# A Fourier mixing and squared-ReLU FFN kernel: self-mirrored frequencies as single tokens, and the odd DFT sums in a PSUM bank of their own

## The chip, the cores and the metric

The kernel runs on one core of a Trainium2 chip. The time is the device time of one execution in microseconds (us); what is compared is the median of several executions. A profile of one execution stands beside it: its span runs from the first to the last instruction and is a little shorter than the device time.

The core has five engines that take their instructions in program order and wait for one another by semaphores. TensorE (PE) does the matmuls and writes into the accumulator memory, PSUM, which this kernel uses as eight banks of 512 float32 columns on 128 partitions. ScalarE (ACT) and VectorE (DVE) read PSUM, do the elementwise work and write to the on-chip memory, SBUF. GpSimd (POOL) does some elementwise work from SBUF to SBUF. SyncE (SP) issues most of the transfers.

## The reference

```python
x: [8, 3008, 256]; w_in: [256, 2048]; w_out: [2048, 256]      # float32
X = np.fft.fft(np.fft.fft(x, axis=1), axis=2).real            # mix over sequence and features
t = X.reshape(8 * 3008, 256)                                  # 24064 tokens
h = np.maximum(t @ w_in, 0.0)
out = (h * h) @ w_out
```

The input is real, so the output rows of the frequencies k and 3008 - k of a batch come from the same two sums, one cosine sum P and one sine sum Q over the sequence: one row is P + Q after the feature transform, the other is P - Q. The kernel works on such a pair as a "plus" token and a "minus" token. The frequencies 0 and 1504 are mirrored to themselves.

## The kernel before

The sizes: M = 1504 is half the sequence, QN = 752, NE = 753 even and NO = 752 odd frequencies from 0 to 1504, so NK = 1505 pairs for each of 8 batches.

**First stage.** The input is folded on DVE, and then a DFT of length 752 is done as matmuls with cosine and sine tables, in two blocks (even and odd frequencies), for each of P (`pt`) and Q (`qt`). A block is a sum over six slices: slices 0, 2, 4 give a sum A, slices 1, 3, 5 a sum B. The lower half of a block's frequencies is A + B; the upper half is B - A (or A - B), read backwards.

```python
def dft_ops(blk, mms, m, fin, run=3):
    ...
        def f():
            ms = mms(par)                                  # par 0: slices 0, 2, 4; par 1: slices 1, 3, 5
            if lo == 0 and par == 0:
                st[0] = psx.tile([P, 512], F32, name="pf", tag="x")[:, 0:n]      # one PSUM bank
            for i in range(lo, hi):
                rows, wt, q, tab = ms[i]
                mm(st[0][0:rows, :], wt(q), tab[k, q, c0 : c0 + n], par == 0 and i == 0, i == len(ms) - 1)
            if hi < len(ms):
                return
            if par == 0:
                st["a"] = asp.tile([P, HE], F32, name="as", tag="as")[:, 0:n]
                act(st["a"][0:m, :], st[0][0:m, :], AF.Copy, bias=0.0,
                    scale=2.0 if fin[0] is None else fin[0])                     # 2A to SBUF
            else:
                fin[1](st["a"][0:m, :], st[0][0:m, :])                           # bank now holds A + B
...
            def f(a2, lo):                                 # fin of stage1_ops
                act(lo_, lo, AF.Copy, bias=0.0, scale=1.0)                       # lower half: ACT copies A + B
                ...
                    vt(hi_, a2, lo, op=ALU.subtract)                             # upper half: DVE
```

The matmuls of the odd slices add onto the even ones' sum in the same bank, and so they come after ACT's copy of 2A. The first block of batch 0 (`stage1_first`) already has its sums in two banks.

**Second stage.** The pairs of all batches are cut into 25 chunks (two of 256 pairs, 22 of 512, and the last of 264), and each chunk into steps over the 2048 hidden features. A step makes a PSUM tile `xb` of pre-activations; ACT applies ReLU for the plus tokens; the minus tokens are made in one of five ways, which a table of letters (KINDS) picks for each step. The kinds "r" and "v" add a third pass over the columns on PE (with the matrix G3) and finish on ACT (r) or DVE (v). The kinds "d", "q" and "p" do without it and build a correction tile T instead: d on DVE; q with a copy on ACT and an add on POOL; p with the edge term X on POOL; all three finish with one custom DVE instruction. The squaring of `h` goes to DVE, or to ACT where a second table (SQA) says so.

```python
def x_take(c, u):                                          # first half of d, q, p
    ...
    if KINDS[c][u] == "q":
        act(T, xb, AF.Copy, bias=0.0, scale=-2.0)
        for i in range(0, n, CH // 2):
            w = slice(i, i + CH // 2)
            nc.gpsimd.tensor_tensor(T[:, w], T[:, w], X[:, w], op=ALU.add)
    else:
        stt(out=T, in0=xb, scalar=-2.0, in1=X, op0=ALU.mult, op1=ALU.add)
...
def x_back(cur):                                           # second half: r and v
    for j in range(nf):
        for (b, i, o, l) in segs:
            mm(xb[:, j, o : o + l], G3[:, fs], PQ[b][1][:, i : i + l], False, True)
```

**Output.** For each tile of 128 tokens 16 matmuls (128 x 128 by 128 x 256) sum over the hidden features into `po`; ACT evicts it to `os`; SP stores the rows. A chunk's output matmuls are spread among the steps of the following chunks. The last chunk has 264 pairs: two tiles of plus tokens, two of minus tokens, and one tile that holds the 8 remaining pairs of both sides.

```python
def mm2_ops(c):
    full = n // P * P
    tiles = [(s, t0, P) for s in range(2) for t0 in range(0, full, P)]
    groups = [tiles[i : i + 2] for i in range(0, len(tiles), 2)]
    if n > full:
        groups.insert(0, [(2, full, n - full)])            # the tile of both sides
    ...
        w = MW if s == 2 else m                            # MW = 65 columns
        mm(st["o"][0:w, j, :], h2v(c, fc // nf)[:, fc % (2 * nf), o : o + w], wout16[:, fc, :],
           fc == 0 and j == 0, fc == NFC - 1)
```

In `rows_out` the minus rows of the frequencies 0 and 1504 are computed and left unstored.

PSUM is shared out as six banks for `xb`, `pf` and the weight products (`psx`) and two for `po` (`pso`).

Of the kernel before, what the change touches and what calls it, by code (L numbers as in the profile page):

```python
# [18 lines left out]
HS = 32.0  # L19
# [5 lines left out]
def kernel(  # L25
# [19 lines left out]
    NK = NE + NO  # L45
    HE = QN // 2 + 1
# [135 lines left out]
    sgn2 = vec("sgn2")  # L182
# [13 lines left out]
    def sgn_vecs():  # L196
        nc.gpsimd.tensor_scalar(out=sgn, in0=pidx, scalar1=P - 1.5, scalar2=None, op0=ALU.is_lt)
        nc.gpsimd.tensor_scalar(out=s3, in0=sgn, scalar1=-2.0, scalar2=None, op0=ALU.mult)
        nc.gpsimd.tensor_scalar(out=sgn, in0=sgn, scalar1=2.0, scalar2=-1.0, op0=ALU.mult, op1=ALU.add)
        nc.gpsimd.tensor_scalar(out=nsgn, in0=sgn, scalar1=-1.0, scalar2=None, op0=ALU.mult)  # L200
        nc.gpsimd.tensor_scalar(out=sgn2, in0=sgn, scalar1=2.0, scalar2=None, op0=ALU.mult)
# [192 lines left out]
    def alloc_pq(b):  # L394
        PQ[b] = tuple(pp.tile([P, NK], F16, name=n, tag=n) for n in ("pt", "qt"))

    def halves(blk, d):
        if blk == 0:
            return d[:, 0:HE], d[:, NE - 1 : HE - 2 : -1]
        return d[:, NE : NE + HO], d[:, NK - 1 : NE + HO - 1 : -1]  # L400

    def dft_ops(blk, mms, m, fin, run=3):
# [4 lines left out]
        def some(par, lo, hi):  # L407
            def f():
                ms = mms(par)
                if lo == 0 and par == 0:  # L410
                    st[0] = psx.tile([P, 512], F32, name="pf", tag="x")[:, 0:n]
                for i in range(lo, hi):
                    rows, wt, q, tab = ms[i]
                    mm(st[0][0:rows, :], wt(q), tab[k, q, c0 : c0 + n], par == 0 and i == 0,
                       i == len(ms) - 1)
                if hi < len(ms):
                    return
                if par == 0:
                    st["a"] = asp.tile([P, HE], F32, name="as", tag="as")[:, 0:n]
                    act(st["a"][0:m, :], st[0][0:m, :], AF.Copy, bias=0.0,  # L420
                        scale=2.0 if fin[0] is None else fin[0])
                else:
                    fin[1](st["a"][0:m, :], st[0][0:m, :])
# [7 lines left out]
    def stage1_ops(b, blk, inline_e=False, run=3):  # L431
# [12 lines left out]
        def fin(sn):  # L444
            def f(a2, lo):
                hi = P - 1 if sn and not inline_e else P
                lo_, hi_ = halves(blk, PQ[b][sn][0:hi])
                act(lo_, lo, AF.Copy, bias=0.0, scale=1.0)
                if sn and inline_e:
                    stt(out=hi_, in0=lo, scalar=nsgn[:, 0:1], in1=a2, op0=ALU.mult, op1=ALU.add)  # L450
                elif sn:
                    vt(hi_, a2, lo, op=ALU.subtract)
                else:
                    vt(hi_, lo, a2, op=ALU.subtract)
            return f

        ops = []
        for sn in range(2):
            ops.append(dft_ops(blk, lists(sn), P - 1 if sn and not inline_e else P,
                               (sgn2[:, 0:1] if sn and inline_e else None, fin(sn)), run))  # L460
        h = [len(o) // 2 for o in ops]
        return ops[0] + ops[1]
# [36 lines left out]
    def e_ops(bs):  # L499
# [7 lines left out]
        def fin(blk):  # L507
            def f(a2, lo):
                lo_, hi_ = halves(blk, est[bs[0]][0][0:nb])
                act(lo_, lo, AF.Copy, bias=0.0, scale=1.0)  # L510
                vt(hi_, lo, a2, op=ALU.subtract)
            return f

        ops = []
        for blk in range(2):
            ops.append(dft_ops(blk, lambda par, blk=blk: [
                (MW, lambda q: ewide((blk * NQ + q) * B + bs[0]), q, cosT)
                for q in range(par, NQ, 2)], nb, (None, fin(blk))))
        return [start] + [o[i] for i in range(2) for o in ops]

    def e_row(b):
        t, i = est[b]
        nc.sync.dma_start(out=PQ[b][1][P - 1 : P, :], in_=t[i : i + 1, :])

    NPAIR = B * NK
# [3 lines left out]
    assert all(n <= CH // 2 or n == CH or n % P < P // 4 for n in sizes)  # L529
    chunks = []  # L530
    g = 0
    for n in sizes:
        segs = []
        o = 0
        while o < n:
            b, i = divmod(g + o, NK)
            l = min(n - o, NK - i)
            segs.append((b, i, o, l))
# [3 lines left out]


    KINDS = ["vrvrrrvrrrrrrrrr"] + ["rvvrvrvrrrrrrrrr"] + ["rvrrvvrrvvvrrrrr"] + ["rrrrrrrrdqqdrrrr"] + ["rdrqdrqdrrrvdrrd"] + ["rrrrdqrrqrqdrqqd"] + ["rrrrrrqqqddrdrqd"] + ["rrdrqpdrpdqrrrqr"] + ["drpddrqrpdqrdrdr"] + ["qdqrqrdrvrddqdrr"] + ["ddrqddprrrddrqdr"] + ["qrqddrqdrrddqprr"] + ["drrdrddrrdpqdrdr"] + ["rqqdrdrqrqqrqddq"] + ["qrdddrqrqdpqqqdq"] + ["rrrrrrqqqddqrdrq"] + ["ddddqrqpqdpqdqrr"] + ["ppdrqdrqrdqdvqqr"] + ["qdqqdqrqrqdqdqvq"] + ["drqddqrddrdqrqpq"] + ["dpdqddqqrrdrqddr"] + ["qdqqdqrdqrqdrdqr"] + ["qdqddqrrdrqdrdqr"] + ["qdqqdqvrqrqdqrdp"] + ["rrppddpddddrppdp"]
    SQA = [(2,)] * 2 + [(1, 6)] + [(1, 4)] + [(0, 2, 3, 5)] + [(0, 6)] + [(1, 3, 7)] + [(2, 6)] + [(0, 2, 5, 7)] + [(0, 2, 4, 7)] + [(3, 7)] + [(0, 2, 4, 6)] + [(0, 2, 5)] + [(2, 4, 6)] + [(1,)] + [(1, 4, 6, 7)] + [(1, 2, 6)] + [(1, 4, 6)] * 2 + [(0, 5, 6, 7)] + [(1, 4, 6)] * 3 + [(1, 4, 6, 7)] + [(0, 1, 2, 6)]

    LEAD = ["2222222222222222"] * 3 + ["2222222246222222"] + ["2325322822222228"] + ["2222462222242224"] + ["2222222262122228"] + ["2252248522227232"] + ["5262823222223242"] + ["2622222222258222"] + ["2272622222222262"] + ["4223722222225622"] + ["2227223222628222"] + ["2226222221228242"] + ["6224422722233722"] + ["2222222282272322"] + ["4222222526636622"] + ["2225222212222242"] + ["8223822222422222"] + ["2242642242482252"] + ["2224282822222222"] + ["2822222222282222"] + ["2222222222222222"] + ["2282222222222222"] + ["2262232122422275"]
    DEFER = ["1111111111111111"] * 3 + ["1111111311131111"] + ["1101011111112111"] + ["1111221111111111"] + ["1111111111111111"] + ["1121113111111111"] + ["1112111111131111"] + ["1111211111121211"] + ["1121111111111121"] + ["1111211311111111"] + ["1111111111111111"] + ["1122101111111211"] + ["1111011111111131"] + ["1111111110111111"] + ["1111111011111111"] + ["1111101211111111"] + ["1111111111211111"] + ["1211101111111010"] + ["1111111111111111"] + ["1111211121131111"] + ["1111311211111111"] + ["1111111111111111"] + ["1101111101113111"]
    SQLAG = ["1111"] + ["3103"] + ["31123133"] + ["33343343"] + ["33332333"] + ["42331333"] + ["33331433"] + ["33333323"] + ["33344033"] + ["33323223"] + ["33333333"] + ["33333233"] * 2 + ["13333022"] + ["33333314"] + ["33333312"] + ["34333333"] + ["32333333"] + ["33232313"] + ["33133133"] + ["33333333"] + ["33233333"] + ["33333333"] + ["33323333"] + ["33334332"]
# [20 lines left out]
    def mm2_ops(c):  # L570
        g0, n, nf, segs = chunks[c]
        full = n // P * P
        tiles = [(s, t0, P) for s in range(2) for t0 in range(0, full, P)]
        groups = [tiles[i : i + 2] for i in range(0, len(tiles), 2)]
        if n > full:
            groups.insert(0, [(2, full, n - full)])
# [3 lines left out]
        def rows_out(s, t0, m, src):  # L580
            base = g0 + n - t0 - m if s else g0 + t0
            o = 0
            while o < m:
                b, i = divmod(base + o, NK)
                if i < NE:
                    l = min(m - o, NE - i)
                    kk = 2 * i
                else:
                    l = min(m - o, NK - i)
                    kk = 2 * (i - NE) + 1  # L590
                lo, hi = 0, l
                if s and kk == 0:
                    lo = 1
                if s and kk + 2 * (l - 1) == M:
                    hi = l - 1
                if hi > lo:
                    if s:
                        r0 = b * S + S - (kk + 2 * (hi - 1))
                        p0 = m - (o + hi)
                    else:  # L600
                        r0 = b * S + kk + 2 * lo
                        p0 = o + lo
                    nl = hi - lo
                    nc.sync.dma_start(out=out[r0 : r0 + 2 * nl - 1 : 2, :], in_=src(p0, nl))
                o += l

        def store(grp, po, js=None):
            os_ = osp.tile([P, 2, D], F32, name="os", tag="os")
            if grp[0][0] == 2:
                _, t0, m = grp[0]  # L610
                act(os_[0 : 2 * m, 0], po[0 : 2 * m, 0], AF.Copy, bias=0.0, scale=HS * HS)
                rows_out(0, t0, m, lambda p0, nl: os_[p0 : p0 + nl, 0, :])
                rows_out(1, t0, m, lambda p0, nl: os_[m + p0 : m + p0 + nl, 0, :])
                return
            js = js or slice(0, len(grp))
            act(os_[:, js], po[:, js], AF.Copy, bias=0.0, scale=HS * HS)  # L616
            for j, (s, t0, m) in list(enumerate(grp))[js]:
                rows_out(s, t0, m, lambda p0, nl, j=j: os_[p0 : p0 + nl, j, :])

        def one(grp, j, fc):  # L620
            s, t0, m = grp[j]

            def f():
                if j == 0 and fc == 0:
                    st["o"] = pso.tile([P, 2, D], F32, name="po", tag="po")
                o = n + n % P + t0 if s == 1 else t0
                w = MW if s == 2 else m
                mm(st["o"][0:w, j, :], h2v(c, fc // nf)[:, fc % (2 * nf), o : o + w], wout16[:, fc, :],
# [14 lines left out]
    def relu_d(c, u, put):  # L643
        n, nf = chunks[c][1:3]
        o = u % 2 * nf
        d = h2v(c, u)[:, o : o + nf, n : 2 * n]
        k = n % P
        if k:
            put(d[:, :, 0:k][:, :, ::-1], slice(0, k))
            put(d[:, :, k:n][:, :, ::-1], slice(k, n))  # L650
# [315 lines left out]
```

## Time and profile before

| what | value |
|---|---|
| time, median of 3 (lowest to highest) | 605.47 us (605.43 to 607.0) |
| span of the profiled execution | 603.7 us |
| mean granted PE clock | 0.994 of full speed |
| output matmuls (`po`, 256 columns) | 3024, 450.4 us busy |
| DFT matmuls (`pf`) in all | 240 |
| ACT copies of even sums (`as`, line 420) | 34, 0.46 to 0.63 us each |
| ACT copies of lower halves (`pt`, `qt`, `es`, lines 448 and 510) | 34, about 0.5 us each |
| DVE subtractions for upper halves (lines 450, 452, 454, 511) | 34, about 0.55 us each |
| squarings of 128 x 2048: DVE / ACT (two halves) | 116 at 1.23 us / 68 at 1.10 + 1.08 us |

Busy time is the sum of an engine's instruction durations. PE's matmuls overlap one another by their run-out, so PE's pace is read from the distance between starts and not from the mean duration of a matmul. "Idle before" is the time an engine stood still just ahead of an instruction, and the releaser is the instruction whose semaphore ended it. PE loads the weights of the next matmul beside the running one; those loads are listed as PEld.

### The profile page before, as it was taken

The page shows a single profiled execution, that of the slowest core. Times are in us where ns is not written, and L with a number is a line of the kernel's source. Part 1 is how long each engine was busy: PE and PEld are TensorE (multiplying, and loading weights), DVE is VectorE, ACT ScalarE, POOL GpSimd, SP SyncE. Part 2 cuts the span into 40 slices and gives each one's busy share as a digit, 9 for nine tenths or more (in the row PEclk, how much of TensorE's full clock was granted, in tenths as well). Part 3 has the DMA queues.
Part 4 walks back from the last instruction along what each step waited for, and adds up shares of the span by engine and source line. Part 5 has one row for each costly group of instructions (what it writes and reads, how often), then busy time and mean ns, then how long its engine had stood idle before and what let it go on. Part 6 is the DMA issues. An engine that isn't in the chain of part 4 may idle for free.

```text
span 603.7 us, 12339 instructions
## 1 busy us (share of the span) xinstructions
PE 579.6 (96%) x4539; PEld 436.3 (72%) x4539; DVE 523.4 (87%) x950; ACT 544.8 (90%) x976; POOL 188.3 (31%) x256
## 2 busy tenths in 40 slices
PE   3869899999999999999999999999999999999997
PEld 1546577777777777777787778777787778877786
DVE  7969698998799899988998988988989889899880
ACT  7868799999989899989999989998999899999981
POOL 6301022223231232323104354153453434324400
PEclk9979999999999999999999999999999999999999
DMA  8974755673584313913133115123242231332112
GB/s 251 298 75 111 157 156 180 210 188 102 56 226 88 44 55 54 256 44 57 46 54 62 35 55 53 54 44 58 58 55 48 42 61 54 44 62 56 55 54 71
DMA packets 41954, 56.25 MB, mean 93 GB/s; under 512 B 7746, under 2 KB 36726, under 8 KB 41894
## 3 DMA queue, kind: packets, MB, share of 16 engines
q1 hardware_dynamic: 37030, 42.04, 32.1%
q0 software_dynamic: 4864, 13.44, 9.0%
q8 instruction: 35, 0.57, 0.4%
q14 instruction: 25, 0.20, 0.1%
HBM read 29.02 MB, written 24.64 MB: 89 GB/s over the span
## 4 chain that ended last, share of the span: by engine, by line
PE 92%; DMA 4%; ACT 1%; POOL 1%; issue 1%; DVE 1%; POOLq 0%; ACTq 0%; DVEq 0%
PE po L74 54%; PE xb L74 31%; PE pf L74 6%; DMA wout<-in_moe_w_out_dram 3%; DMA x<-in_x_dram,idx 1%; POOL x L99 0%; POOL x L112 0%; ACT as L420 0%; ACT os L616 0%; ACT h L726 0%; DVE w L375 0%; DVE v L371 0%; ACT h L747 0%; DVE sinT L304 0%; DVE cosT L304 0%
## 5 line engine op out<-in xcount | busy, mean ns | idle before, releaser
L74 PE MATMUL po<-wout,h 128*128 128x256 f16 x3024 | 450.4, 273 | 4.8 <-DMA wout<-in_moe_w_out_dram 4.3
L74 PEld LDWEIGHTS <-h 128*128 128x128 f16 x3024 | 286.8, 98 | 113.5 <-issue 5.6
L714 POOL TENSOR_TENSOR bs<-bs,h 128x256 f32<-128x256 f32 x190 | 141.0, 764 | 289.3 <-ACT bs L711 225.4
L74 PE MATMUL xb<-qt,G 128*128 128x512 f16 (+10 forms) x737 | 205.2, 322 | 0.4 <-DVE qt L487 0.3
L727 DVE CUSTOM_DVE_ANT_0 h<-xb,bs 128x512 f16<-128x512 f32 (+1 forms) x237 | 147.9, 638 | 19.6 <-ACT h L726 14.9
L726 ACT ACTIVATE h<-xb 128x512 f16<-128x512 f32 (+1 forms) x224 | 139.4, 625 | 11.6 <-PE xb L74 9.9
L74 PE MATMUL xb<-pt,G 128*128 128x512 f16 (+16 forms) x512 | 146.7, 324 | 0.6 <-ACT h L738 0.3
L750 DVE TENSOR_TENSOR h<-h 128x2048 f16<-128x2048 f16 (+1 forms) x120 | 144.6, 1209 | 0.2
L74 PEld LDWEIGHTS <-G 128*128 128x128 f16 x1249 | 119.9, 98 | 23.8 <-issue 1.7
L669 ACT ACTIVATE h<-xb 128x512 f16<-128x512 f32 (+1 forms) x160 | 100.2, 630 | 8.9 <-PE xb L74 8.5
L716 DVE SCALAR_TENSOR_TENSOR bs<-xb,h 128x512 f32<-128x512 f32 (+1 forms) x129 | 84.9, 659 | 17.6 <-PE xb L74 13.9
L738 ACT ACTIVATE h<-xb 128x512 f16<-128x512 f32 (+2 forms) x145 | 89.7, 621 | 6.7 <-PE xb L74 5.2
L748 ACT ACTIVATE h<-h 128x1024 f16<-128x1024 f16 (+1 forms) x72 | 77.4, 1076 | 0.0
L747 ACT ACTIVATE h<-h 128x1024 f16<-128x1024 f16 (+1 forms) x72 | 76.3, 1059 | 0.1
L695 DVE TENSOR_SCALAR h<-eb,gE 128x512 f16<-128x512 f16 (+1 forms) x203 | 69.5, 360 | 0.3 <-DMA eb<-qt 0.2
L616 ACT ACTIVATE os<-po 128x512 f32<-128x512 f32 (+1 forms) x95 | 59.6, 627 | 8.9 <-PE po L74 8.9
L711 ACT ACTIVATE bs<-xb 128x512 f32<-128x512 f32 x95 | 59.6, 627 | 2.0 <-DVE h L727 1.0
L112 POOL DMA_INDIRECT x<-in_x_dram,idx x16 | 18.2, 1138 | 80.4 <-DVE u L366 63.3
L362 DVE TENSOR_TENSOR u<-x 127x765 f16<-127x765 f32 x32 | 29.7, 948 | 1.2 <-DMA x<-in_x_dram,idx 1.2
L74 PEld LDWEIGHTS <-w 127*128 127x128 f16 (+1 forms) x192 | 21.7, 117 | 8.4 <-issue 2.5
L375 DVE TENSOR_TENSOR w<-v 127x384 f16<-127x384 f16 x64 | 23.0, 383 | 0.0
L74 PE MATMUL pf<-cosT,w 127*128 127x377 f16 (+1 forms) x96 | 20.6, 323 | 2.2 <-ACT as L420 1.1
(111 smaller groups left out, 216.9 us busy)
## 6 DMA issues: line engine op xcount, KB each, us to landing
out_dram<-os SPq DMA_DIRECT2D x157, 128.0 KB
x<-in_x_dram SPq DMA_DIRECT2D x16, 756.0 KB
wst<-in_moe_w_in_dram SPq DMA_DIRECT2D x4, 512.0 KB
eb<-qt SPq DMA_DIRECT2D x14, 128.0 KB
wout<-in_moe_w_out_dram POOLq DMA_DIRECT2D x4, 256.0 KB, 17.3
x<-in_x_dram,idx POOLq DMA_INDIRECT x20, 10.5
gE<-G SPq DMA_DIRECT2D x16, 0.2 KB
x<-in_x_dram SPq DMA_DIRECT2D x14, 2.0 KB
```

What stands on the lines that cost most here:

```text
L74: nc.tensor.matmul(o, l, r, start=start, stop=stop, skip_group_check=True)
L616: act(os_[:, js], po[:, js], AF.Copy, bias=0.0, scale=HS * HS)
L669: act(r_s(c, u), xb, AF.Relu, scale=-1.0)
L695: ts(out=X, in0=ebc[c][:, 0:n], scalar1=gE2[:, u : u + 1], scalar2=None, op0=ALU.mult)
L714: nc.gpsimd.tensor_tensor(T[:, w], T[:, w], X[:, w], op=ALU.add)
L716: stt(out=T, in0=xb, scalar=-2.0, in1=X, op0=ALU.mult, op1=ALU.add)
L726: act(r_s(c, u), xb, AF.Relu, scale=-1.0)
L727: mirrors.append((int(DEFER[c][u]), lambda: relu_d(c, u, lambda o, i: nc.vector._custom_dve(TENSOR_ADD_SAT, out=o[:, 0, :], in0=xb[:, 0, i ...
L738: relu_d(c, u, lambda o, i: act(o, xb[:, :, i], AF.Relu, scale=-1.0))
L747: act(h2[:, 0:nf], h2[:, 0:nf], AF.Square)
L748: rest.append(lambda: act(h2[:, nf:], h2[:, nf:], AF.Square))
L750: vt(h2, h2, h2, op=ALU.mult)
```

## The change

Two things are changed, and the tables that place the work are set anew.

First, the frequencies 0 and 1504 of every batch are taken out of the pairs. Their columns of P and Q are copied aside by POOL (`self_copy`), and the 16 columns of the 8 batches are put behind the pairs of the last batch (`self_append`), as plus tokens without a minus token. The pairs are now 1503 for each batch; the last chunk has 248 pairs and 16 single tokens, 512 tokens in all. The odd tile of both sides and its handling go.

Second, the odd sums of a DFT get a bank of their own. ACT still copies A (now with scale 1, or with a sign) to SBUF; DVE makes both halves, A + B and B - A, and ACT's copy of the lower half goes.

Beside these, POOL's add of a "q" step is one instruction over 512 columns in place of two, and KINDS, SQA, three tables of delays and the places of the folds and DFTs among the steps are changed.

```diff
-    def halves(blk, d):
+    selfs = [const.tile([P, NS], F16, name=n) for n in ("ptS", "qtS")]        # NS = 16
+    def self_copy(b):
+        for sn in range(2):
+            hi = P - 1 if sn and b not in INL else P
+            nc.gpsimd.tensor_copy(selfs[sn][0:hi, 2 * b : 2 * b + 2], PQ[b][sn][0:hi, 0 : NE : NE - 1])
+    def self_append():
+        for sn in range(2):
+            nc.gpsimd.tensor_copy(PQ[B - 1][sn][:, NT : NT + NS], selfs[sn])
+    def halves(blk, d, o=None):                 # the odd block now begins at column NE - 1
 ...
     def dft_ops(blk, mms, m, fin, run=3):
-                if lo == 0 and par == 0:
-                    st[0] = psx.tile([P, 512], F32, name="pf", tag="x")[:, 0:n]
+                if lo == 0:
+                    st[par] = psx.tile([P, 512], F32, name="pf", tag="x")[:, 0:n]
-                    mm(st[0][0:rows, :], wt(q), tab[k, q, c0 : c0 + n], par == 0 and i == 0,
+                    mm(st[par][0:rows, :], wt(q), tab[k, q, c0 : c0 + n], i == 0,
                        i == len(ms) - 1)
-                        scale=2.0 if fin[0] is None else fin[0])
+                        scale=1.0 if fin[0] is None else fin[0])
-                    fin[1](st["a"][0:m, :], st[0][0:m, :])
+                    fin[1](st["a"][0:m, :], st[1][0:m, :])
 ...
-            def f(a2, lo):
+            def f(a, bp):
-                act(lo_, lo, AF.Copy, bias=0.0, scale=1.0)
                 if sn and inline_e:
-                    stt(out=hi_, in0=lo, scalar=nsgn[:, 0:1], in1=a2, op0=ALU.mult, op1=ALU.add)
-                elif sn:
-                    vt(hi_, a2, lo, op=ALU.subtract)
+                    stt(out=lo_, in0=a, scalar=sgn[:, 0:1], in1=bp, op0=ALU.mult, op1=ALU.add)
+                    later(lambda: stt(out=hi_, in0=bp, scalar=nsgn[:, 0:1], in1=a, op0=ALU.mult,
+                                      op1=ALU.add))
                 else:
-                    vt(hi_, lo, a2, op=ALU.subtract)
+                    vt(lo_, a, bp, op=ALU.add)
+                    if sn:
+                        vt(hi_, a, bp, op=ALU.subtract)
+                    else:
+                        later(lambda: vt(hi_, bp, a, op=ALU.subtract))
 ...
     def e_row(b):
-        nc.sync.dma_start(out=PQ[b][1][P - 1 : P, :], in_=t[i : i + 1, :])
+        nc.sync.dma_start(out=PQ[b][1][P - 1 : P, 0 : NE - 1], in_=t[i : i + 1, 0 : NE - 1])
+        nc.sync.dma_start(out=PQ[b][1][P - 1 : P, NE - 1 : NT], in_=t[i : i + 1, NE:NK])
+        nc.sync.dma_start(out=selfs[1][P - 1 : P, 2 * b : 2 * b + 2], in_=t[i : i + 1, 0 : NE : NE - 1])
-    NPAIR = B * NK
+    NPB = NT - 1                                # 1503
+    NPAIR = B * NPB + NS
 ...
     def mm2_ops(c):
-        full = n // P * P
-        tiles = [(s, t0, P) for s in range(2) for t0 in range(0, full, P)]
+        n1 = mirrored(c)                        # n, less 16 in the last chunk
+        tiles = list(range(0, n + n1, P))
-        if n > full:
-            groups.insert(0, [(2, full, n - full)])
 ...
-            for i in range(0, n, CH // 2):
-                w = slice(i, i + CH // 2)
-                nc.gpsimd.tensor_tensor(T[:, w], T[:, w], X[:, w], op=ALU.add)
+            nc.gpsimd.tensor_tensor(T, T, X, op=ALU.add)
 ...
     warm_up(10)
+    gcast(0, nc.scalar.copy)
     hi_ops = []
     s1 = stage1_first(hi_ops)
     s1[0]()
     warm_up(0)
-    gcast(0, nc.scalar.copy)
 ...
-    spread(fo, 12, 13)
+    spread(fo, 9, 10)
     spread(tr1[0:5], 12, 13)
-    spread(tr1[5:], 12, 13)
+    spread(tr1[5:], 11, 12)
-    FOLD = {0: [(1, 0.511, 0.793)], ...
+    FOLD = {0: [(1, 0.475, 0.842)], ...         # the fold of batch 1, as shares of batch 0's steps
-    ST1 = {0: (0.9, 0.99)}
+    ST1 = {0: (0.843, 0.905)}                   # the DFT of batch 1
+    side.setdefault(first_step[B - 1] + 5, []).append(self_append)
```

The tables, summed over all 400 steps (and, for SQA, over all pairs of steps):

| | r | v | d | q | p | squarings on ACT |
|---|---|---|---|---|---|---|
| before | 158 | 18 | 108 | 95 | 21 | 72 |
| after | 168 | 14 | 106 | 92 | 20 | 79 |

## The prediction

> **What bounds the kernel now.** I read the page first, for the share of each engine and the slices; then the busy time by stretch, to see where TensorE (PE) is not full; then PE's waits, which name what it stood for; then PE's timeline of two places, the end of the start-up and the tail.
>
> From the page (busy time and share of the span; then the same in 40 slices, in tenths):
> ```profile
> PE 579.6 (96%) x4539; PEld 436.3 (72%) x4539; DVE 523.4 (87%) x950; ACT 544.8 (90%) x976; POOL 188.3 (31%) x256
> ...
> PE   3869899999999999999999999999999999999997
> ```
> The stretches (length, then busy time and number of instructions of PE, PEld, DVE, ACT, POOL):
> ```profile
> 36.00:75.00 39.00, 35.79 (x235) 24.26 (x234) 29.00 (x58) 29.13 (x56) 2.23 (x2) 0.95 0.51 108
> 75.00:150.00 75.00, 75.00 (x587) 54.17 (x585) 70.55 (x128) 71.39 (x128) 21.50 (x24) 1.00 0.57 168
> 150.00:300.00 150.00, 150.00 (x1200) 112.21 (x1198) 134.02 (x230) 140.15 (x245) 40.53 (x51) 1.00 0.44 92
> 300.00:450.00 150.00, 150.00 (x1206) 115.69 (x1204) 134.32 (x235) 140.60 (x251) 57.32 (x78) 1.00 0.30 53
> ```
> From 75 us to 580 us PE has no gap: that part lasts as long as its matmuls, and a shorter ACT or DVE instruction there buys nothing by itself. Everything else is in the first 75 us and the last 24 us. What PE stood for:
> ```profile
> PE warm L74 <- POOL ez L341: 9.3, 1, 9.3
> PE po L74 <- DMA wout<-in_moe_w_out_dram: 4.3, 1, 4.3
> PE pf L74 <- ACT as L420: 2.5, 4, 0.7
> PE pc L74 <- ACT win L323: 1.9, 1, 1.9
> PE pf L74 <- DVE sinT L304: 0.7, 1, 0.7
> PE po L74 <- ACT os L616: 0.5, 1, 0.5
> ```
> (total us, times, longest). Rows one, two and four lie before 36 us. Row three is what the change aims at: four times the odd sums of a DFT waited until ACT had copied the even sums out of the same bank. One of the four, in PE's timeline:
> ```profile
> 63.01 0.65 PE L74 MATMUL pf<-cosT,w 127*128 127x377 f16 x3
> 64.23 0.64 PE L74 MATMUL pf<-cosT,w 127*128 127x377 f16 x3 [0.57 <-ACT as L420]
> ```
> Three such matmuls are issued in 0.48 us elsewhere in the timeline (65.19 to 65.67), so the second trio could have begun at 63.49 and began at 64.23: 0.74 us lost, more than the 0.57 us booked as idle, because the last matmul's run-out counts as busy. The tail, from the chain of work that ended last:
> ```profile
> 586.50 11.37 PE po L74 x104
> 597.94 0.39 ACT os L616
> 598.38 1.92 PE po L74 x16
> ```
> After 586.5 us only output matmuls are left, 120 of them, one every 11.37 / 104 = 0.1093 us, with one break for an eviction.
>
> **What the Trainium skill says.** "TensorE: Matmul & The Clock Gate", section "Back-to-back issue gap", gives 262 cycles for 256 columns and 518 for 512, 0.109 and 0.216 us at its 2.4 GHz. The trace agrees: 0.1093 us above, and 0.22 us from one 512-column matmul to the next instruction (199.66 to 199.88 us). "Perfetto Trace Analysis", section "Matmuls", says that independent groups should go through different PSUM banks, so that the eviction of one lies beside the matmuls of the next. The four waits above are what the old form pays for not doing so. "TensorE: Matmul & The Clock Gate", section "HAM oscillation", says that an idle stretch over about 3.4 us halves the clock afterwards. The trace agrees: after the 4.3 us wait for the output weights four output matmuls take 0.81 us at 35.57 us, against 0.44 later. The change doesn't touch this, so I leave that cost as it is. "GPSIMD Engine Reference", section "Elementwise — side-by-side cycle accounting", has 4497 ns for a 2048-element float32 add; with the trace's 764 ns for 256 elements a straight line gives an estimate of 1.3 us for one 512-wide add, against 2 x 764 ns = 1.53 us for the two halves.
>
> **The change part by part.**
>
> *1. No token twice.* Before, each batch gives 1505 plus and 1505 minus tokens, though frequencies 0 and 1504 mirror to themselves: 24080 tokens for 24064 rows, so 188 full tiles and one odd tile of 65 columns, 16 output matmuls more. After, 8 x 1503 pairs and 16 single tokens make 24064 = 188 x 128. The odd tile falls in the last chunk, whose output matmuls all lie in the tail where PE runs alone: 16 x 0.1093 = **-1.75 us**. The tail's last eviction and its store stay. The elementwise work of the last chunk gets lighter (thirteen 8-wide DVE pieces of 159 ns vanish, -2.1 us of DVE), but PE has 40 matmuls of the chunk before to do then (120 less 80), so this brings nothing more.
>
> *2. More triple-pass steps.* Kinds "r" and "v" make the mirrored half with a third pass over the columns; "q", "d" and "p" don't. Counted in the two tables, before has 158 + 18 = 176 of the former, after 168 + 14 = 182. All six are in full 512-column chunks, inside the stretch where PE has no gap: 6 x 0.216 = **+1.29 us**.
>
> *3. Odd sums in a bank of their own.* The number of DFT matmuls stays. The four waits in the early part can go. Counted by start times as above: 0.89 (45.71 to 47.08 less 0.48), 0.74, 0.74 and 0.83: 3.2 us. The rescheduling also moves the odd fold of batch 0 from step 12 to step 9 and the later sine and cosine activations from 12 to 11, which makes the 0.84 us gap at 43.92 (for sinT) likely to go: **up to -4.0 us**. Later DFTs have no such wait today, because other matmuls lie between the halves.
>
> *4. What it costs elsewhere.* ACT loses 34 low-half copies (30 of about 0.50 us, 4 of 0.47): -17 us. DVE gains 34 adds of about 0.545 us: +18.5 us. The tables pay that back. DVE: 4 fewer v, 2 fewer d, 3 fewer q, 1 fewer p, at 0.68, 1.73, 1.04 and 1.37 us each, -10.7 us; 7 squarings go to ACT, -8.6 us at 1.23; with part 1, about -3 us in all. ACT: 10 more r at 0.635 us, 3 fewer q copies at 0.63, 7 squarings at 1.10 + 1.08 us, so +6.4 - 1.9 + 15.2 - 17, less 1 in the last chunk: about +2 us. So DVE would stay near 520 us and ACT near 546: the balance in the stretch from 75 to 580 us is kept, and both remain under PE.
>
> *5. Small things.* 16 tiny GpSimd copies and two appends, one fewer sign vector, three row transfers instead of one for six batches, one 512-wide GpSimd add in place of two. GpSimd is busy 31% of the time. The cast of the first input-weight quarter moves in the program ahead of matmuls only; no ACT instruction lies between its old place and its new one, so the 1.9 us wait stays, as does that for the output weights.
>
> Sum without new waits: -1.75 + 1.29 - 4.0 = -4.5 us.
>
> **Rivals.**
>
> *A new wait for PSUM.* The pool has six banks. A DFT took one and now takes two, and the first DFTs come in bursts (all of batch 0's odd block in one step). Each bank is held for less time than before, but the next step's bank comes up sooner. For it: DVE, which now makes both halves, is 87% busy, and before 47.49 us it sat in 2.35 us of squarings that stood ahead of such a subtraction. The last of these subtractions ended at 49.36, and the next matmul over that block began at 49.56, so there is 0.2 us of room. Against it: the fold is earlier, and DVE has fewer v steps in chunks 1 and 2. If it were to bite at every one of 34 DFTs with 0.2 us, it would eat 7 us and give about 608. I charge 0.8 us for the early part and 0.4 us for the rest.
>
> *DVE waits for GpSimd.* The small copy of the self-mirrored columns must come before the odd block overwrites one of them, and it stands in GpSimd's queue behind adds that wait for ACT. For it: GpSimd's waits on ACT are the longest in the table (225 us in all). Against it: in steady state the overwrite comes several steps after the copy. Worth 0 to 2 us, around 604.
>
> *The gain is hidden.* If what follows the early DFTs is bound by DVE or by the fold of batch 1 (now up to 0.842 of its span with the DFT starting at 0.843, so with no room between), the 4 us turn into other waits, and only parts 1 and 2 remain: -0.5 us, 605. For it: the DFT of batch 1 began 3 steps after its fold, and now follows at once. Against it: the DFT is also one to two steps earlier, with room before its first use.
>
> *ACT becomes the bound.* It is at 93.5% in 150 to 300 us; 2 us more over 500 us is not enough.
>
> **Range and chances.** -4.5 + 1.2 = -3.3 gives 602.2 us. The low end takes all of the 4 us and a little from the start, 600.0. The high end takes the third rival with some of the first, 605.8. A change of 2% is 12 us: more than all gaps after 36 us together (3.2 + 0.5 by the wait rows), so faster by that much is all but ruled out; slower by it would need new gaps in most of the DFTs.
>
> **What would show it.** Right: no row "PE pf <- ACT as"; 3008 output matmuls, and about 104 rather than 120 after the last xb matmul; PE idle in 36 to 75 us under 1.5 us rather than 3.2; still no gap from 75 to 580; DVE near 520 and ACT near 546 us. Wrong: waits of xb or pf on DVE (pt, qt, as), a PE share below 100% around the DFTs, or a later landing of the output weights than 35.5 us, which would shift everything behind it.

## The result and the profile after

The changed kernel takes **601.68 us** (median of four, 600.74 to 602.27) against 606.07 us for the kernel before, measured on the same chip; the ratio is 0.9925 with a 95% interval of 0.9903 to 0.9947. The span of the profiled execution went from 603.7 to 600.4 us.

The page after, busy time by engine and the 40 slices of PE:

```profile
PE 579.4 (96%) x4529; PEld 436.2 (73%) x4529; DVE 524.5 (87%) x946; ACT 548.1 (91%) x959; POOL 170.7 (28%) x174
...
PE   3879999999999999999999999999999999999997
```

The shares are those of before: PE full, DVE 87%, ACT 91% for 90%. In time DVE rose by 1 us and ACT by 3, so the new tables did keep the balance. What moved must be read from the waits. PE's waits after (total us, times, longest):

```profile
PE warm L76 <- POOL ez L341: 9.3, 1, 9.3
PE po L76 <- DMA wout<-in_moe_w_out_dram: 3.4, 1, 3.4
PE pc L76 <- ACT win L323: 2.0, 1, 2.0
PE xb L76 <- ACT h L679: 0.9, 3, 0.6
PE po L76 <- ACT os L633: 0.5, 1, 0.5
PE xb L76 <- DVE h L735: 0.4, 1, 0.4
```

The rows "pf <- ACT as" (2.5 us, four times) and "pf <- DVE sinT" (0.7 us) are gone. Two small rows are new or longer: 0.9 us on ACT's ReLU (0.6 us of it at 32.45 us, ahead of the first output matmul) and 0.4 us on DVE's mirrored half. The DFT that stood for 0.74 us at 63.49 in the kernel before now runs through; PE's timeline:

```profile
60.94 1.13 PE L76 MATMUL pf<-cosT,w 127*128 127x377 f16 x6
61.91 0.65 PE L76 MATMUL pf<-cosT,ez 127*128 127x377 f16 x3
```

Six matmuls, even and odd sums, begin within 0.97 us, which is their bare pace. The tail, from the chain of work that ended last:

```profile
585.19 9.62 PE po L76 x88
594.81 0.03 ACTq L633
594.83 0.05 issue
594.88 0.39 ACT os L633
595.27 0.04 issue
595.32 1.92 PE po L76 x16
```

That is 104 output matmuls for 120, and 9.62 us for 11.37 in front of the eviction: 1.75 us.

To see where time was lost and not only where PE was idle, I gave each matmul of the trace its bare pace: a 256-column one 0.1093 us and a 512-column one 0.216 us, so 2.6 ns and 0.4168 ns for each column. What a stretch lasts beyond the sum of these is lost to waits, run-outs and a halved clock. A matmul counts in the stretch in which it starts.

| lost time of PE, us | 0 to 34 | 34 to 80 | 80 to 580 | from 580 | bare pace, all matmuls |
|---|---|---|---|---|---|
| before | 18.3 | 7.8 | 1.2 | 4.3 | 572.1 |
| after | 17.6 | 5.3 | 1.8 | 4.1 | 571.6 |

So 0.5 us of the gain is fewer columns, the sum of 16 output matmuls less and six third passes more. Another 3.2 us is time no longer lost before 80 us and 0.2 us at the end, less 0.6 us newly lost in the middle. The border at 34 us lies inside the wait for the output weights. Cut at the first output matmul instead (35.57 us before, 36.89 us after), the loss is 19.9 and 20.5 us ahead of it, and 6.2 and 2.4 us from there to 80 us.

### The profile page after: what moved, and what is told of

Its sections match the earlier page's. It is cut to its first block, busy times and chain, and to the rows that moved or that the text cites. A ratio compares the mean times of both kernels' runs of the same rounds, so it can differ in the third digit from the quotient of the medians.

```text
span 600.4 us, 12229 instructions
## 1 busy us (share of the span) xinstructions
PE 579.4 (96%) x4529; PEld 436.2 (73%) x4529; DVE 524.5 (87%) x946; ACT 548.1 (91%) x959; POOL 170.7 (28%) x174
## 4 chain that ended last, share of the span: by engine, by line
PE 88%; DMA 4%; ACT 4%; issue 1%; POOL 1%; DVE 1%; ACTq 0%; POOLq 0%; DVEq 0%
PE po L76 52%; PE xb L76 31%; PE pf L76 6%; DMA wout<-in_moe_w_out_dram 3%; DMA x<-in_x_dram,idx 1%; ACT h L734 1%; ACT h L755 1%; ACT h L756 0%; ACT os L633 0%; ACT bs L721 0%; POOL x L101 0%; POOL x L114 0%; DVE h L735 0%; DVE h L705 0%; DVE bs L724 0%
## 5 line engine op out<-in xcount | busy, mean ns | idle before, releaser
L76 PE MATMUL xb<-qt,G 128*128 128x512 f16 (+10 forms) x743 | 208.0, 323 | 1.2 <-ACT h L679 0.9
L722 POOL TENSOR_TENSOR bs<-bs,h 128x512 f32<-128x512 f32 x92 | 118.3, 1289 | 308.3 <-ACT bs L721 247.7
L735 DVE CUSTOM_DVE_ANT_0 h<-xb,bs 128x512 f16<-128x512 f32 (+1 forms) x218 | 143.5, 666 | 22.6 <-ACT h L734 19.4
L734 ACT ACTIVATE h<-xb 128x512 f16<-128x512 f32 (+1 forms) x218 | 135.1, 621 | 8.3 <-PE xb L76 6.0
L758 DVE TENSOR_TENSOR h<-h 128x2048 f16<-128x2048 f16 (+1 forms) x113 | 138.2, 1224 | 0.8 <-ACT h L746 0.7
L679 ACT ACTIVATE h<-xb 128x512 f16<-128x512 f32 (+1 forms) x166 | 103.8, 629 | 9.6 <-PE xb L76 8.7
L746 ACT ACTIVATE h<-xb 128x512 f16<-128x512 f32 (+1 forms) x152 | 95.4, 629 | 10.3 <-PE xb L76 8.5
L724 DVE SCALAR_TENSOR_TENSOR bs<-xb,h 128x512 f32<-128x512 f32 (+1 forms) x126 | 82.9, 659 | 20.0 <-PE xb L76 16.3
L756 ACT ACTIVATE h<-h 128x1024 f16<-128x1024 f16 (+1 forms) x79 | 84.6, 1071 | 0.0
L755 ACT ACTIVATE h<-h 128x1024 f16<-128x1024 f16 (+1 forms) x79 | 83.5, 1056 | 0.0
L721 ACT ACTIVATE bs<-xb 128x512 f32<-128x512 f32 x92 | 57.3, 623 | 2.9 <-PE xb L76 1.1
L114 POOL DMA_INDIRECT x<-in_x_dram,idx x16 | 21.0, 1313 | 61.1 <-DVE u L366 49.0
L76 PE MATMUL pf<-sinT,w 127*127 127x377 f16 (+1 forms) x96 | 20.9, 323 | 0.0
## 6 DMA issues: line engine op xcount, KB each, us to landing
wout<-in_moe_w_out_dram POOLq DMA_DIRECT2D x4, 256.0 KB, 18.1
```

The costliest lines, as they stand in the source:

```text
L76: nc.tensor.matmul(o, l, r, start=start, stop=stop, skip_group_check=True)
L679: act(r_s(c, u), xb, AF.Relu, scale=-1.0)
L722: nc.gpsimd.tensor_tensor(T, T, X, op=ALU.add)
L734: act(r_s(c, u), xb, AF.Relu, scale=-1.0)
L735: mirrors.append((int(DEFER[c][u]), lambda: relu_d(c, u, lambda o, i: nc.vector._custom_dve(TENSOR_ADD_SAT, out=o[:, 0, :], in0=xb[:, 0, i ...
L746: relu_d(c, u, lambda o, i: act(o, xb[:, :, i], AF.Relu, scale=-1.0))
```

## The experiments

The theory: PE's columns and PE's waits in the first 75 us set the time, so the parts add: tokens -1.75 us, six third passes +1.29 us, second banks some -3 us. The rivals: that new waits on DVE take the place of the old ones; that the new tables are the price of the second bank; that the tail is set by stores. Each run was timed in five rounds beside the kernel before on the same chip. "Before" in a comparison is that round's own median.

**The second bank for the early DFTs only.**

```diff
 # the kernel before; six DFTs of batches 0 and 1: own = b in INL
-                if lo == 0 and par == 0:
-                    st[0] = psx.tile(...)
+                if lo == 0 and (own or par == 0):
+                    st[par if own else 0] = psx.tile(...)
 ...
+                if own:                       # DVE makes both halves
+                    vt(lo_, a2, lo, op=ALU.add); vt(hi_, lo, a2, op=ALU.subtract); return
                 act(lo_, lo, AF.Copy, bias=0.0, scale=1.0)
```

> The kernel before, with one edit: the six DFTs of batches 0 and 1 that had their odd sums in the even sums' bank get a second bank, and DVE makes both halves there; all tables and places as before. If the four waits of PE on ACT were worth what their start times say, 3.2 us go and the rest stays: about 602.9 us against 606.1 for the kernel before, PE idle in 36 to 75 us down from 3.2 to about 0.7 (the sinT gap stays). The rival, that DVE and the fold bound this part anyway, expects no gain (605 to 606 us) and new waits of PE on DVE (pt or qt) in the same stretch.

Measured: 603.34 us against 606.25, ratio 0.9939 (0.9920 to 0.9959): -2.9 us. PE's waits on the early DFTs, all that is left of them:

```profile
PE xb L74 <- DVE qt L451: 0.4, 1, 0.4
```

No "pf <- ACT as" is left, and the gap before sinT has gone as well, which I had expected to stay. I had misread it. In the kernel before, the matmul at 44.76 us waits for a semaphore of DVE and for one of ACT, and both came at the same moment, while the view names only one of them:

```profile
44.21 0.50 ACT L420 ACTIVATE as<-pf 128x376 f32<-128x376 f32 x1
44.44 0.27 DVE L304 TENSOR_SCALAR sinT<-sinT,alt 128x188 f16<-128x188 f16 x1
```

In this run, with its own bank, the same DFT runs through its six matmuls with cosT while sinT is still being written:

```profile
44.33 1.12 PE L74 MATMUL pf<-cosT,w 127*128 127x376 f16 x6
44.90 0.26 DVE L304 TENSOR_SCALAR sinT<-sinT,alt 128x188 f16<-128x188 f16 x1
```

So the kernel before had five waits on a shared bank, 4.0 us by start times, and not four and one for a table. From the first output matmul to 80 us the lost time fell from 6.2 to 3.6 us: the five waits, less 0.6 us of a halved clock that lasted longer here and two new short gaps, 0.6 us by start times on DVE (the row above) and 0.3 us. The rival that DVE bounds this part is out.

**The tokens alone.** The changed kernel with the old DFT form and all old tables and places, which is the kernel before with the token part.

> The kernel before with only the token part of the change: self-mirrored frequencies as 16 single tokens, 188 full tiles; the odd sums in the even sums' bank, and all tables and places as before. If the saving is 16 output matmuls in the tail, 1.75 us go: about 604.3 us, with 104 instead of 120 output matmuls after the last xb matmul, and the four PE waits on ACT stay. The rival, that the tail is set by the last evictions and stores, expects no change (606 us).

Measured: 606.76 us against 606.25, ratio 1.0006 (0.9994 to 1.0019): no gain. The rival named the wrong place, though. The tail did shrink:

```profile
588.22 9.62 PE po L76 x88
```

but it began at 588.22 rather than 586.50. In the profile more was waited for before it, and by lost time PE fell behind by 0.6 us from 34 to 80 us and by 1.1 us from 80 to 580 us:

```profile
PE pf L76 <- ACT as L435: 3.7, 6, 0.7
PE pf L76 <- DVE w L377: 2.2, 2, 1.9
PE xb L76 <- DVE pt L471: 0.7, 1, 0.7
```

Six waits on ACT's copy instead of five, and one on DVE between 300 and 450 us. The small copy aside had taken a place of its own among the DFT steps and had moved all the others, so that odd sums followed even ones more closely and halves came later. The wait for w stands at the very start, before anything of the token part has been computed; it differs between executions, and here a shorter wait for the input weights (0.2 us for 1.9) made up for it.

**The tokens alone, places kept.** That idea was tried by hanging the copy on the first DFT step.

```diff
-        ops = [lambda: self_copy(b)] if blk else []
+        ops = []
 ...
+        if blk:
+            first = ops[0]
+            ops[0] = lambda: (self_copy(b), first())
```

> The kernel before with only the token part, as in the earlier run, but with the small copy of the self-mirrored columns hung on the first DFT step instead of taking a place of its own among them, so that the DFTs of each batch stand where they stand in the kernel before. If the missing 1.75 us of the earlier run were lost because the DFT steps had moved, the waits of PE go back to four on ACT, the one on DVE between 300 and 450 us goes, and the time is about 604.5 us. If the copy itself, or its wait, is what costs, the waits stay and so does 606 to 607 us.

Measured: 603.80 us against 605.63, ratio 0.9972 (0.9963 to 0.9982): -1.8 us, the 1.75 us of the 16 matmuls. PE has no gap from 75 to 580 us again; the early waits on ACT remain (3.7 us in the same five). The copy costs nothing; its place among the DFT steps did.

**The second bank everywhere, old tables.** The edit of the early banks with `own = True`, and the same for the four DFTs of the edge row.

> The kernel before with a second bank for the odd sums of all 34 DFTs and both halves on DVE, tokens and all tables and places as before. DVE goes from 523 to about 542 us busy, ACT from 545 to about 528. If PE is the bound with room to spare, this is as good as the early banks alone, about 602.9 us, and the six extra three-pass steps and seven squarings moved to ACT were not needed. If DVE has no such room, PE gets gaps between 75 and 580 us, waiting for DVE, and the time is 605 us or more: then the new tables are the price of the second bank.

Measured: 603.50 us against 606.25, ratio 0.9945 (0.9925 to 0.9966). The page:

```profile
PE 581.7 (96%) x4539; PEld 436.6 (72%) x4539; DVE 538.9 (89%) x984; ACT 533.1 (88%) x942; POOL 188.4 (31%) x256
```

DVE took the 15.5 us and still PE lost only 1.3 us from 80 to 580 us, for 1.2 before the change. So 28 more DFTs in second banks bring nothing and cost nothing that can be told from 0, and the six third passes were not the price of the bank.

**The old DFT form in the changed kernel.**

```diff
-                    st[par] = psx.tile(...)          # and lower half on DVE
+                    st[0] = psx.tile(...)            # only for the even sums; lower half copied by ACT
```

> The changed kernel with the old DFT form put back: odd sums in the even sums' bank, lower half copied by ACT; tokens, tables and places as in the changed kernel. The four waits come back, +3.2 us: about 604.9 us against 601.7 for the changed kernel. ACT goes from 548 to about 565 us busy; if ACT has no room for that, PE gets gaps on ACT between 75 and 580 us and the time is 606 us or more.

Measured: 612.76 us against 606.25, ratio 1.0103 (1.0080 to 1.0125): 11 us above the changed kernel, where the five waits would be 4.0 us. PE's waits:

```profile
PE pf L76 <- ACT as L435: 4.8, 6, 1.4
PE po L76 <- DMA wout<-in_moe_w_out_dram: 3.0, 2, 2.7
PE xb L76 <- DVE h L734: 2.2, 5, 0.6
```

and lost time of 10.6 us from 34 to 80 us and 7.2 us from 80 to 580 us. ACT is 558.3 us busy. The new tables give ACT ten more mirrored halves and seven squarings; that there is no room for them without the 17 us that the second bank took off ACT is argued from this, and what DVE waited for from 80 to 580 us fits it:

```profile
DVE pt L471 <- ACT pt L465: 14.0, 8, 3.0
```

With the rows of `qt` (8.8 us) and `es` (4.3 us) that is 27 us of waiting for ACT's copies of lower halves, against 11 us in the tokens run. So PE's rows name DVE where DVE itself came late. Part of this run's lateness comes from the copies' place in the steps, but the tokens run has the same DFT form and the same place, and took 606.76 us: the new tables and places make 6.0 us of the difference here, and nothing beside the second bank, as the next run shows. The tables are no price of the bank, but they do need it.

**Both parts, all old tables and places.** KINDS, SQA, the three delays, the folds and the DFT of batch 1 as in the kernel before.

> The changed kernel (tokens and banks) with all tables and places of the kernel before: KINDS, SQA, the three delays, the folds and the DFT of batch 1. If only the two parts of the change count and the new tables bring nothing, it is the all-banks run less the token part's 1.75 us: about 601.8 us, equal to the changed kernel. If the new tables were needed for the two parts together, PE shows gaps between 75 and 580 us and the time is above 603 us.

Measured: 601.67 us against 605.63, ratio 0.9929 (0.9917 to 0.9942). That is the changed kernel's 601.68: the retuning as a whole is worth nothing. The gap that I had laid to sinT is gone with the old places too. By lost time the retuned kernel saves 1.4 us before 80 us, some of it in the wait for the output weights, which differs between executions, and pays 1.3 us for the six third passes. The small copy has a place of its own among the DFT steps here too, and with the second bank no cost of it shows: the all-banks run less 1.75 us is 601.75.

**Fewer third passes in the changed kernel.** First KINDS alone was put back:

> The changed kernel with only the KINDS table of the kernel before: six steps fewer that pass a third time over the columns, 176 instead of 182. If the middle is bound by PE's columns alone, 6 x 0.216 = 1.3 us go: about 600.4 us against 601.7 for the changed kernel, with no new gap of PE between 75 and 580 us. The rival, that the six were needed so that DVE and ACT keep up, expects gaps there that cost as much or more: 601.7 us or above.

Measured: 600.46 us against 605.63, ratio 0.9919 (0.9906 to 0.9932). In this run the delays belong to other kinds of steps, and part of its output is not the reference's; that some correction tiles are overwritten before they are read is likely and was not traced. The instructions are all there. So it was run again with the delays that belong to that table:

> The changed kernel with four tables of the kernel before, KINDS and the three delays that belong to it (LEAD, DEFER, SQLAG): 176 three-pass steps instead of 182, while the squarings on ACT and the places of the folds and DFTs stay as changed. If PE's columns alone set the middle, 6 x 0.216 = 1.3 us go: about 600.4 us. The rival, that DVE and ACT then lag, expects gaps of PE between 75 and 580 us and 601.7 us or more.

Measured: 600.94 us against 606.31, ratio 0.9915 (0.9902 to 0.9929). By medians 0.7 us less than the changed kernel, but the intervals overlap, so the time alone leaves 1.3 us or nothing open. The trace is clearer: the bare pace of all matmuls falls by 1.3 us, to 570.4 us, and the middle loses 2.2 us for 1.8. The six passes cost their columns, and without them the middle lost about a third of that again.

**Keeping PE busy through the wait for the output weights.**

```diff
+        if take and not warmed:              # just ahead of the first output matmul
+            w2 = psx.tile([P, 512], F32, name="warm", tag="x")
+            for _ in range(12):
+                mm(w2, ez[:, 1, 0, :], ez[:, 1, 0:4, :], True, True)
```

> The changed kernel with 12 idle matmuls of 512 columns (2.6 us) on PE just ahead of the first output matmul, in the 3.4 us in which PE waits for the output weights. If that wait is what halves PE's clock afterwards (output matmuls 0.21 us apart from 36.9 to about 41.5 us), keeping PE busy saves about 2 us: 599.7 us. The rival, that the clock there falls for another reason or that the idle matmuls only delay the first real one, expects 601.7 us or a little more.

Measured: 601.77 us, no gain. The idle matmuls read a buffer that DVE was still writing, and PE stood still before them instead; the timeline:

```profile
34.65 4.21 PE L76 MATMUL warm<-ez 128*128 128x512 f16 x12 [2.12 <-DVE ez L382]
38.69 0.60 PE L76 MATMUL po<-wout,h 128*128 128x256 f16 x4
```

The first output matmuls did run at full pace (0.60 us for four, 1.01 without), 1.8 us later than in the changed kernel (36.89). The halved clock fell on the idle matmuls: 12 of them took 4.04 us, 0.34 us each for a bare pace of 0.216. The second attempt, on the kernel with the old step tables, used operands that were ready and 14 idle matmuls:

> The run with the old step tables, plus 14 idle matmuls of 512 columns (3.0 us) ahead of the first output matmul, now on operands that are ready (the feature matrix and G1), so that PE has no gap of its own before them. If keeping PE busy keeps its clock, the first output matmuls are 0.11 us apart and about 2 us go: 598.5 us against 600.4. The rival, that the clock falls all the same or the idle matmuls hold up the first real one, expects 600.4 us or more.

Measured: 600.63 us against 600.94 without them: nothing that can be told from 0. The clock stayed whole, and PE now waited for each of the first three quarters of the weights:

```profile
36.20 0.60 PE L76 MATMUL po<-wout,h 128*128 128x256 f16 x4 [1.17 <-DMA wout<-in_moe_w_out_dram]
...
37.47 0.60 PE L76 MATMUL po<-wout,h 128*128 128x256 f16 x4 [0.46 <-DMA wout<-in_moe_w_out_dram]
...
38.97 0.60 PE L76 MATMUL po<-wout,h 128*128 128x256 f16 x4 [0.46 <-DMA wout<-in_moe_w_out_dram]
...
43.12 1.12 PE L76 MATMUL pf<-cosT,w 127*128 127x376 f16 x6
```

The same two places in the run without idle matmuls:

```profile
34.85 1.01 PE L76 MATMUL po<-wout,h 128*128 128x256 f16 x4 [4.03 <-DMA wout<-in_moe_w_out_dram]
...
43.38 1.12 PE L76 MATMUL pf<-cosT,w 127*128 127x376 f16 x6
```

In both, the first output matmul begins as the first quarter lands (36.15 and 34.81 us). From there to the next DFT PE took 6.9 us with the whole clock and 8.5 us with the halved one. By start distances the halved clock had cost 2.6 us; of these 0.9 us went into the waits for the second and third quarter, and 1.6 us was saved. It did not show in the profiled time because the first quarter landed 1.3 us later in this execution; from that DFT to the end both take 555.7 us. With the order of issue unchanged and no idle matmuls, the first output matmul lies between 34.9 and 37.6 us among the profiles here, and what sets this is not known. So the halved clock is not shown to be free: what a whole one is worth with the same landing was not measured.

**The output weights ahead of batch 1's input.** On the kernel with the old step tables:

```diff
+    load_w_out()
     for f in rd1[0:0] + fe[1][0:3] + [lambda: load_x(1)] + fe[1][3:]:
         f()
-    load_w_out()
```

> The run with the old step tables, with the four transfers of the output weights issued ahead of the loads of batch 1 instead of behind them. If the wait for them (3.4 us, and some 2 us of halved clock after it) is only a matter of the order of issue, both go and the time is about 595.5 us. The rival, that all early transfers share one full set of DMA engines so that the input weights come later by as much, expects the gap to move to the input weights (20 us) or to the fold of batch 1, and 599 to 602 us.

Measured: **597.97 us** against 606.31, ratio 0.9852 (0.9837 to 0.9866), the fastest of all, with nothing of the computation left out. Issue moves from 18.7 to 10.7 us, and the first output matmul begins at 32.24 us:

```profile
PE po L76 <- DVE h L758: 1.5, 1, 1.5
PE pc L76 <- ACT win L323: 1.4, 1, 1.4
PE pf L76 <- DVE w L375: 1.4, 1, 1.4
```

No wait for the output weights is left, nor a halved clock (lost time from 34 to 80 us: 2.1 us for 4.2). A 1.5 us wait for a squaring has come forward in its place, and a wait for w, 1.4 us, stands at the start, where that kernel's other run had no such row; DVE stood 2.8 us instead of 0.8 for batch 0's input. Whether the early transfers caused this second wait is not shown, since with the old order it lies between nothing and 2.5 us among the profiles here. That the early transfers share what there is, as the rival said, shows in the weights themselves: issued 8 us earlier, their first quarter landed 14 us earlier, but the other three only 3 to 5 us (at 30.9, 33.9 and 36.0 us for 36.1, 37.5 and 39.0). The two waits are about as long as what is missing of the 5 us that I had expected; 3.0 us came.

## Why the prediction was right

**The tokens, -1.75 us.** Confirmed: the tail is shorter by 9.62 for 11.37 us, and the part alone gave -1.8 us once the DFT steps stood where they had stood.

**The six third passes, +1.29 us.** Their columns are there, as counted: the bare pace of all matmuls fell by 0.45 us net, where -1.75 + 1.29 says 0.46. The reason I gave for taking PE as the only limit of the middle held too; the kernel without them has a bare pace 1.3 us lower and gains 0.7 us by its median, which the noise leaves open.

**The second bank, up to -4.0 us.** From the first output matmul to 80 us the lost time fell from 6.2 to 2.4 us, so 3.8 of the 4.0 us came; the early banks alone gave 2.9 us of time. The mechanism was right for more than I had given it: the 0.84 us at 43.92 us was not a wait for sinT that the rescheduling removes but a fifth wait on a shared bank. It is gone in all three runs with second banks and the old places, where the six matmuls of that DFT begin without a gap (at 44.33, 45.17 and 44.24 us). I had put it into this term for a wrong reason, and it was luck that the sum came out unharmed. Ahead of the first output matmul 0.7 us more was lost: it came at 36.89 for 35.57 us, with six more 256-column matmuls (0.66 us) done ahead of it, since the output weights landed later in this execution (18.1 us after issue for 17.3). I had left that wait as it is; among the profiles here it lies between 2.4 and 5.5 us with no system that I could name, so 1 us of any single difference is of this kind.

**The engines' balance.** DVE came out at 524.5 us, not 520; ACT at 548.1, not 546.

**The rivals.** I had charged 0.8 us for new PSUM and DVE waits in the early part and 0.4 us for the rest. The rest lost 0.6 us more, 0.5 us of it in two waits at 456 and 495 us. In the early part no such wait came; what took its place in the sum was the 0.7 us of the later weights, and that is luck again. GpSimd did not hold anyone up for long: its copies took 0.36 to 0.40 us on average, and DVE stood 0.3 us for one of them; its single 512-wide add took 1289 ns on average, which is the estimate of 1.3 us.

**What stayed open: the halved clock.** I took the slow output matmuls after the weights' wait for a cost of their own, outside the change. They were that: by start distances the halved clock cost 2.0 us before and 2.2 us after. The runs with idle matmuls leave open how much of it could be had.

Sum as it came, in the two profiled executions: -0.5 (columns) - 3.2 (before 80 us) + 0.6 (middle) - 0.2 (end) = -3.3 us of span, 603.7 to 600.4. The prediction's -3.3 was the same sum with another charge. That the two agree to 0.1 us is chance: by medians the gain is 4.4 us, and the interval of the ratio allows 3.2 to 5.9.

## What to carry to other kernels

Where PE has no gap, count columns and nothing else; where it has gaps, read them by the distance between starts, not by the idle column, and look at which of them a change removes. Where a matmul waits for two engines and the profile names one, look when the other was done. Adding into a bank that another engine still reads cost 0.7 to 0.9 us here wherever no other matmuls lay between, so give early and bunched groups a second bank and leave the spread-out ones. A new small step in a hand-placed schedule should hang on an existing one: beside the old DFT form, taking a slot of its own cost as much as the whole token part gained.

## What was not expected of the hardware

A wait of over 3.4 us, which the prediction named as what halves the clock, was not needed for it. The longest wait for the output weights was 2.1 us in the all-banks run and 2.7 us in the old DFT form in the changed kernel. In both, the first four output matmuls still ran at full pace, 0.11 us apart, and the clock fell 0.6 and 1.4 us after the first of them: the granted clock reads 0.50 from 38.3 to 41.5 us in the one and from 38.2 to 41.4 us in the other, and 1.00 just before.

The order of issue of the early transfers was worth 3.0 us: the four quarters of the output weights took 16 to 18 us to land behind the other loads, and 10 to 23 us when they were issued 8 us earlier.
